# Backward pass of two attention and two gated feed-forward layers: the remaining turned gradient blocks come from transposing loads

## The chip, the cores and the metric

One program runs on one core of a Trainium2 chip. The core has TensorE (matmuls, PE in the profile, with its weight loads listed as PEld), VectorE (DVE), ScalarE (ACT), GpSimd (POOL) and SyncE (SP), which issues every transfer of this kernel from one queue (SPq); sixteen transfer engines carry the transfers out. The metric is the device time of one execution in microseconds, and lower is better. Matmul results land in PSUM, of which this kernel uses eight banks under the names t, g, u (two each), y and ln (one each).

## The reference

The reference runs a network of four layers forward and then returns the output and the gradients of the input and of all weights. It alternates a linear attention layer A and a gated feed-forward layer B, each behind a layer norm and with a residual. There are 2048 rows of 512 features, all in bf16.

```python
def _B_ref(x, w_gate, w_up, w_down):          # F = 1376
    g = jnp.einsum("bsd,df->bsf", x, w_gate)
    u = jnp.einsum("bsd,df->bsf", x, w_up)
    h = _sigmoid(g) * u
    return jnp.einsum("bsf,fd->bsd", h, w_down)
...
x = A_x
x = x + _A_ref(_layernorm(x, axis=-1), A_wqkv, A_wo)
x = x + _B_ref(_layernorm(x, axis=-1), B_w_gate, B_w_up, B_w_down)
x = x + _A_ref(_layernorm(x, axis=-1), A_wqkv, A_wo)
x = x + _B_ref(_layernorm(x, axis=-1), B_w_gate, B_w_up, B_w_down)
...
_out, _vjp = jax.vjp(_f, A_x, A_wqkv, A_wo, B_w_gate, B_w_up, B_w_down)
_grads = _vjp(grad_out)
```

The part that matters here is the gradient through `_B_ref`. With G the gradient of the layer's output, the gradient of h is G times w_down transposed. The matmul of TensorE contracts over the partitions, so G must be at hand turned, with its 512 features on partitions; this turned copy is the tile `gT`.

## The kernel before

The kernel runs the four layers forward and then backwards: the feed-forward gradient stage of layer 3 (the first such stage, 393 to about 500 us of the profile), the attention gradient of layer 2 with the weight gradients of layer 3 as filling, the feed-forward gradient stage of layer 1 (the second, from about 713 us), the attention gradient of layer 0, and the last weight gradients.

A feed-forward gradient stage is the class `BBwd`; its method `run` (L1507) goes through four blocks B of four row tiles each (512 rows), and in each block through eleven units u of 128 columns of F. Both stages together have eight blocks. For a unit, `D` (L1448) computes the gradient of h into a PSUM bank g (`dhh_ps`, four matmuls that stream all 512 rows of `gT`, L1461), ScalarE copies it to `dhb` (L1467), and VectorE and GpSimd multiply it with two factors `ssd` saved by the forward pass (L1468, L1469) into `dd`. `H` (L1485) then adds eight matmuls for that unit to four accumulators (`dh_ps`, L1493). `D` runs two units ahead of `H`. `R` turns `dd` on VectorE and stores it for the weight gradients (`tr_stg`, L1090, L1093). At a block's last unit `ln_begin` reads the four accumulators on ScalarE and VectorE (L1293, L1312), and the next block writes the same four banks. The loads of `ssd` come in groups of three units (two in the last) into two buffers (L1442), each load when the group two before it has been used; `h_ld` (L1446) is the saved row data for the layer norm's gradient, and `gstage` holds G in row layout.

There are two ways to fill `gT`, which has two buffers (and one more, `pre_gT`, for block 0 of the first stage). `turn_g` (L1407) issues two transposing loads of 256 rows each, from the input grad_out in the first stage (it is the gradient itself there) and from the stored rows `sv_gbf` in the second, which `cast_g` (L1415) has written. `make_gT` (L1423) turns 256 rows by eight TensorE transposes of `gstage` into a PSUM bank and one copy on ScalarE. Before the change the first stage uses loads for blocks 0 and 1 (`GTURN = 2`) and TensorE for blocks 2 and 3, in units 5 and 6 of block 1 and in units 7 and 8 of block 2; the second stage uses TensorE for block 0 and loads for blocks 1 to 3, each asked for at unit 0 of the block before.

The second stage begins while the weight gradients of layer 3 (`p2_gen`, L1722) still run. These are jobs of four units; a unit is sixteen matmuls into `p_ps` (L1778) and one copy out. A job reads a set `p_set` (L1655, L1662 or L1647) from two buffers; the next load of a set goes out when the job that used its buffer has ended. The last job is taken inside `run`: three units, then the transposes of block 0, then the fourth unit.

PE, ACT, DVE and POOL follow the order written in the program within these stages (`tc.manual_schedule(engines=EM)`). SP is not in that set: the framework places its transfers. `tc.issue_after` puts one transfer behind another by hand, as for the weights of the second stage (L247) and its first two `ssd` loads. The hook at block 1, unit 0 of the second stage (`open_w2`, L289) loads MT (L251) and the first sets of the next weight gradients.

Of the kernel before, what the change touches and what calls it, by code (L numbers as in the profile page):

```python
# [9 lines left out]
BF16 = mybir.dt.bfloat16  # L10
# [12 lines left out]
P = 128  # L23
NST = S // P
NDC = D // P
# [11 lines left out]
NBLK = NST // NB  # L37
BT = NB * P
# [22 lines left out]
def ps_tile(k, which, shape, dt, name):  # L61
    return k.ps[which].tile(shape, dt, name=name, tag="ln_tp" if which == "ln" else f"{which}_ps")
# [327 lines left out]
def dram_batch(ap2d, b, nb=NB):  # L390
    return ap2d[batch_rows(b, nb), :].rearrange("(n p) d -> p n d", p=P)
# [978 lines left out]
UNIT = [(g, u - c0, nch) for g, (c0, nch) in enumerate(CG) for u in range(c0, c0 + nch)]  # L1370


GTURN = 2


class BBwd:


# [18 lines left out]
    def load_g(self, B):  # L1397
        if B >= NBLK:
            return
        k, nc = self.k, self.k.nc  # L1400
        t = self.G[B] = self.G.get(B) or self.alloc(False, "stg", [P, NB, D], "gstage", 2)
        if self.first:
            if B < GTURN:
                self.turn_g(B)
            nc.sync.dma_start(out=t[:], in_=dram_batch(k.g_in, B))

# [8 lines left out]
    def cast_g(self, B, j):  # L1415
# [3 lines left out]
        nc.scalar.copy(self.G[B][:, j, :], k.xs[B * NB + j][:])  # L1419
        if j == NB - 1:  # L1420
            nc.sync.dma_start(out=dram_batch(self.sv["gbf"], B), in_=self.G[B][:])

    def make_gT(self, B, half, bank="ln"):  # L1423
        if B >= NBLK:
            return
        k, nc = self.k, self.k.nc
        if half == 0 and B not in self.gT:
            self.gT[B] = self.alloc(False, "work", [P, NDC, BT], "gT", 2)
        ps = ps_tile(k, bank, [P, NDC, 2, P], BF16, "gT_ps")
        for j in range(2):  # L1430
            for c in range(NDC):
                nc.tensor.transpose(ps[:, c, j, :], self.G[B][:, half * 2 + j, c * P:(c + 1) * P], k.ident[:])
        nc.scalar.copy(self.gT[B][:, :, half * 2 * P:(half + 1) * 2 * P], ps[:].rearrange("p c n t -> p c (n t)"))

    def load_ssd(self, n):
        B, g = divmod(n, len(CG))
# [70 lines left out]
    def run(self, nxt, hooks={}, rest=None, fill=None):  # L1507
        k, nc, tc, l = self.k, self.k.nc, self.k.tc, self.l
        if not self.first:
            k.load_b_weights([rest.R.dmas[i] for i in (-6, -5, -3, -3, -2, -1)])  # L1510
        with ExitStack() as ctx:
            for nm, bufs in (("ld", 2), ("stg", 2), ("work", 2), ("tr", 3)):
                self.p[nm] = ctx.enter_context(tc.tile_pool(name=f"bb_{nm}{l}", bufs=bufs, reuse_waits="tile"))
            self.small = ctx.enter_context(tc.tile_pool(name=f"bb_small{l}", bufs=4, reuse_waits="tile"))
            ctx.enter_context(tc.manual_schedule(engines=EM))
            if self.first:
                for n in (1, 2):
                    self.load_ssd(n)
            else:
                self.load_g(0)  # L1520
                with tc.issue_after(rest.R.dmas[-1]):
                    for n in range(2):
                        self.load_ssd(n)
                for j in range(NB):
                    self.cast_g(0, j)
                self.G[1] = self.alloc(False, "stg", [P, NB, D], "gstage", 2)
                for j in range(NB):
                    self.cast_g(1, j)
                if rest is not None:
                    rest.take(rest.left - 1)  # L1530
                self.make_gT(0, 0)
                self.make_gT(0, 1, "g")
                if rest is not None:
                    drain(rest)
            if self.first:
                self.load_g(1)
            for n in range(self.LOOK):
                self.D(n)
                self.R(n)
            self.D(self.LOOK)  # L1540
            self.R(self.LOOK)
            lns = None
            for B in range(NBLK):
                end = B == NBLK - 1
                for u in range(NFC):
                    n = B * NFC + u
                    close = u == NFC - 1
                    if close and end:
                        nxt.gT_make(0, "ln")
                    behind = self.first and B == 2 and u == 9  # L1550
                    if not close and not behind:
                        self.D(n + self.LOOK)
                    self.H(B, u)
                    if behind:
                        self.D(n + self.LOOK)
                    if close and not end:
                        done = self.ln_begin(B)
                        for i in range(2):
                            self.D(n + self.LOOK + i)
                    if u:  # L1560
                        self.R(n + self.LOOK)
                    if close and not end:
                        self.R(n + self.LOOK + 1)
                    if lns is not None:
                        for j, step in LNSTEPS[u]:
                            getattr(lns[j], step)()
                    if not end:
                        if not self.first and u == 0:
                            self.turn_g(B + 1)
                            if B + 2 < NBLK:  # L1570
                                self.load_g(B + 2)
                        if 1 <= u <= NB:
                            self.cast_g(B + 2, u - 1)
                        late = self.first and B == 2
                        if late and u == 3:
                            self.load_g(3)
                        if u in ((7, 8) if late else (5, 6)) and self.first and B + 1 >= GTURN:
                            self.make_gT(B + 1, 0 if u in (5, 7) else 1)
                    if u in (7, 8):
                        self.load_h(B, u - 7)  # L1580
                    if u == 8 and self.first and B != 1:
                        self.load_g(B + 2)
                    if (B, u) in hooks:
                        fill = hooks[B, u]() or fill
                    if end and u == 9:
                        nxt.begin()
                if not end:
                    lns = done
            lns = self.ln_begin(B, (0, 1))
            next(fill)  # L1590
            lns += self.ln_begin(B, (2, 3))
            nxt.gT_make(1, "ln")
            nxt.dp_make(0)
            next(fill)
            for x in lns:
                x.add()
            nxt.start()
# [14 lines left out]
def drain(gen):  # L1612
    for _ in gen:
        pass
# [575 lines left out]
```

## Time and profile before

| | us |
|---|---|
| median of 3 runs | 1104.92 (1104.79 to 1106.0) |
| the profiled execution | 1104.22 |
| its span, first to last instruction | 1102.5 |
| busy: TensorE, VectorE, ScalarE, GpSimd | 1076.6, 719.1, 484.9, 463.1 |
| transposes of `make_gT` (L1432) | 48 |
| its copies on ScalarE (L1433) | 6 |
| transposing loads of `turn_g` (L1412) | 10 |

In a timeline row the columns are the start in us from the span's start, the length in us, the engine, the line, the operation, the tiles written and read, the shape and the number of merged instructions; in square brackets stands the idle time of the engine before it and what ended it. SPq rows are issues: the length is the time that the queue was held by the issue, and the landing comes later. A row of a table by stretches has the stretch, the busy time of PE, PEld, DVE, ACT and POOL (with instructions), the granted clock of TensorE, the share of the sixteen transfer engines and GB/s.

### The profile page before, as it was taken

To read this page: it belongs to the slowest core of one execution; us is meant where nothing else is said; L and a number is where in the kernel's file an instruction comes from. 1 tells how busy PE (TensorE), PEld (TensorE's weight loads), DVE (VectorE), ACT (ScalarE), POOL (GpSimd) and SP (SyncE) were. 2 spreads that over 40 slices of the span, in tenths; PEclk is the share of its full clock that TensorE was granted. 3 is DMA by queue.
4 is the path that set the end of the run, shared out by engine and by line. 5 is a ranking of instruction groups with operands and counts; after the bars stand their busy time and mean duration, and the time that the engine had idled before them with its cause. 6 is when DMAs were issued, how large, how long until landed. Compare 5 with 4: busy or idle time off the path is not lost. (4 is left out here: it accounts for less than half of the span.)

```text
span 1102.5 us, 19826 instructions
## 1 busy us (share of the span) xinstructions
PE 1076.6 (98%) x7255; PEld 660.9 (60%) x7356; DVE 719.1 (65%) x1257; ACT 484.9 (44%) x907; POOL 463.1 (42%) x631
## 2 busy tenths in 40 slices
PE   8999999999999999999999999999999999999998
PEld 4477777447777744445756556544447755555587
DVE  7798997878888667777965620067778946632221
ACT  6676555547555524444633441234346513420001
POOL 5637776435765447773101420048881102420000
PEclk9999999999999999999999999999999999999999
DMA  8948997796797688976899968898869999958997
GB/s 260 318 150 216 249 251 231 208 251 155 219 290 230 188 273 287 300 237 209 244 269 258 273 212 283 253 334 250 233 189 247 272 256 264 263 184 285 266 253 168
DMA packets 365330, 269.55 MB, mean 244 GB/s; under 512 B 132464, under 2 KB 339760, under 8 KB 365232
## 3 DMA queue, kind: packets, MB, share of 16 engines
q1 hardware_dynamic: 365232, 268.28, 85.3%
q8 instruction: 57, 0.93, 0.3%
q14 instruction: 41, 0.34, 0.1%
HBM read 122.62 MB, written 119.47 MB: 220 GB/s over the span
## 5 line engine op out<-in xcount | busy, mean ns | idle before, releaser
L1778 PE MATMUL p_ps<-p_set,p_a 128*128 128x384 bf16 (+2 forms) x1792 | 264.4, 303 | 1.5 <-DMA p_set<-sv_hdd 0.8
L1778 PEld LDWEIGHTS <-p_a 128*128 128x128 bf16 x1792 | 168.8, 96 | 85.0 <-PE p_ps L1778 1.0
L1469 POOL TENSOR_TENSOR dd<-dhb,ssd 128x512 bf16<-128x512 bf16 x84 | 97.0, 1158 | 102.9 <-ACT dhb L1467 96.3
L1468 DVE TENSOR_TENSOR dd<-dhh_ps,ssd 128x512 bf16<-128x512 f32 x85 | 57.2, 679 | 119.9 <-ACT dhb L1467 117.1
L1493 PE MATMUL dh_ps<-wuT,dd 128*128 128x512 bf16 (+1 forms) x339 | 128.5, 379 | 0.5
L1493 PE MATMUL dh_ps<-wgT,dd 128*128 128x512 bf16 (+1 forms) x329 | 124.7, 379 | 0.1
L1493 PEld LDWEIGHTS <-dd 128*128 128x128 bf16 x680 | 66.4, 98 | 79.6
L1152 POOL TENSOR_TENSOR ssd_t<-hhT,oms 128x512 bf16<-128x512 bf16 (+2 forms) x76 | 82.8, 1098 | 49.1 <-DVE hhT L1151 22.4
L1793 DVE TENSOR_TENSOR dw_stg<-p_ps,dw_stg 128x384 bf16<-128x384 f32 (+2 forms) x76 | 32.2, 438 | 105.6 <-PE p_ps L1778 96.7
L1467 ACT CAST dhb<-dhh_ps 128x512 bf16<-128x512 f32 x84 | 48.7, 589 | 115.4 <-PE dhh_ps L1461 108.1
L1133 PE MATMUL u_ps<-hT,wu 128*128 128x256 bf16 (+1 forms) x792 | 92.7, 261 | 1.2 <-DVE hhT L1151 1.0
L1133 PE MATMUL g_ps<-hT,wg 128*128 128x256 bf16 (+1 forms) x792 | 92.8, 261 | 0.7 <-DVE den L972 0.4
L1090 DVE STREAM_TRANSPOSE tr_stg<-dd 128x768 f32<-128x768 f32 (+1 forms) x62 | 86.8, 1435 | 1.5 <-DMA sv_hdd<-tr_stg 0.4
L1133 PEld LDWEIGHTS <-wg 128*128 128x128 bf16 x792 | 70.1, 98 | 17.0 <-issue 0.5
L1461 PE MATMUL dhh_ps<-gT,wdT 128*128 128x512 bf16 x299 | 76.9, 379 | 2.2 <-DVE dd L1468 1.5
L1168 PE MATMUL y_ps<-wd,hhT 128*128 128x512 bf16 (+1 forms) x337 | 77.7, 379 | 0.8
L1133 PEld LDWEIGHTS <-wu 128*128 128x128 bf16 x792 | 70.6, 98 | 9.0 <-issue 2.1
L1149 ACT ACTIVATE ssd_t<-g_ps 128x512 bf16<-128x512 f32 (+2 forms) x76 | 42.5, 559 | 63.2 <-PE g_ps L1133 60.6
L1795 ACT CAST dw_stg<-p_ps 128x384 bf16<-128x384 f32 (+2 forms) x76 | 28.1, 386 | 84.1 <-PE p_ps L1778 80.9
L1461 PEld LDWEIGHTS <-wdT 128*128 128x128 bf16 x352 | 34.2, 98 | 43.3 <-issue 3.5
L1151 DVE TENSOR_TENSOR hhT<-u_ps,ssd_t 128x512 bf16<-128x512 f32 (+2 forms) x76 | 47.2, 629 | 17.8 <-PE u_ps L1133 11.0
L1150 ACT ACTIVATE oms<-g_ps 128x512 bf16<-128x512 f32 (+2 forms) x96 | 53.7, 559 | 10.0 <-POOL ssd_t L1152 9.3
(256 smaller groups left out, 1879.8 us busy)
## 6 DMA issues: line engine op xcount, KB each, us to landing
sv_hdd<-tr_stg SPq DMA_DIRECT2D x72, 384.0 KB, 4.8
p_set<-sv_hdd SPq DMA_DIRECT2D x18, 1536.0 KB, 7.3
ssd<-sv_ssd SPq DMA_DIRECT2D x23, 768.0 KB, 5.2
sv_ssd<-ssd_t SPq DMA_DIRECT2D x61, 256.0 KB, 3.4
h_ld<-sv_h SPq DMA_DIRECT2D x30, 256.0 KB, 4.0
sv_hdl<-tr_stg SPq DMA_DIRECT2D x24, 256.0 KB, 5.1
p_a<-sv_h SPq DMA_DIRECT2D x12, 512.0 KB, 6.7
p_set<-sv_hdl SPq DMA_DIRECT2D x24, 256.0 KB, 5.0
```

The costliest lines, as they stand in the source:

```text
L1090: nc.vector.transpose(t[:, :, 0:n * P].bitcast(F32).rearrange("p q (a j) -> p q a j", a=2 * n), src.rearrange("p c x -> p (c x)").bitcast( ...
L1133: nc.tensor.matmul(ps[:, ci * n:(ci + 1) * n], lhsT=w_sb[:, kc, (c0 + ci) * P:(c0 + ci + 1) * P], rhs=hT[:, kc, (st % 2) * P:(st % 2) * P ...
L1150: nc.scalar.activation(oms, gv, ACT.Sigmoid, scale=-1.0)
L1151: nc.vector.tensor_tensor(hh, uv, ssd[:, :, 0, :], ALU.mult)
L1152: nc.gpsimd.tensor_tensor(ssd[:, :, 1, :], hh, oms, ALU.mult)
L1168: nc.tensor.matmul(y_ps[:], lhsT=h[0:r, fc, off:off + P], rhs=k.wd[0:r, fc, :], start=(fc == 0), stop=(fc == NFC - 1))
L1461: nc.tensor.matmul(ps[:], lhsT=k.wdT[:, jc, u * P:(u + 1) * P], rhs=self.gT[B][:, jc, :], start=(jc == 0), stop=(jc == NDC - 1))
L1467: nc.scalar.copy(dhb[:], ps[:])
L1468: nc.vector.tensor_tensor(self.dd[ng][:, 0, c, :], ps[:], self.ssd[ng][:, c, 0, :], ALU.mult)
L1469: nc.gpsimd.tensor_tensor(self.dd[ng][:, 1, c, :], dhb[:], self.ssd[ng][:, c, 1, :], ALU.mult)
L1493: nc.tensor.matmul(self.acc[j][:], lhsT=dd[0:r, a, c, j * P:(j + 1) * P], rhs=w[0:r, u, :], start=(u == 0 and a == 0), stop=(u == NFC - 1 ...
L1778: nc.tensor.matmul(ps[:, 0:w], lhsT=lhs[:, s, ic * P:(ic + 1) * P], rhs=rhs, start=(s == 0), stop=(s == NST - 1))
```

## The change

`make_gT` and `GTURN` go. In the first stage blocks 0 and 1 are turned by loads as before; block 2's load is asked for in block 0 behind unit 3, and block 3's in block 2 behind unit 1. The special order of `D` and `H` at block 2, unit 9, goes too. In the second stage the four units of the last job are taken in a row, then block 0's turn is asked for by `turn_g`; blocks 1 to 3 stay as they were. The loads of G in row layout stay in both stages.

```diff
-GTURN = 2
...
-            if B < GTURN:
+            if B < 2:
                 self.turn_g(B)
...
-    def make_gT(self, B, half, bank="ln"):
-        if B >= NBLK:
-            return
-        k, nc = self.k, self.k.nc
-        if half == 0 and B not in self.gT:
-            self.gT[B] = self.alloc(False, "work", [P, NDC, BT], "gT", 2)
-        ps = ps_tile(k, bank, [P, NDC, 2, P], BF16, "gT_ps")
-        for j in range(2):
-            for c in range(NDC):
-                nc.tensor.transpose(ps[:, c, j, :], self.G[B][:, half * 2 + j, c * P:(c + 1) * P], k.ident[:])
-        nc.scalar.copy(self.gT[B][:, :, half * 2 * P:(half + 1) * 2 * P], ps[:].rearrange("p c n t -> p c (n t)"))
...
-                if rest is not None:
-                    rest.take(rest.left - 1)
-                self.make_gT(0, 0)
-                self.make_gT(0, 1, "g")
-                if rest is not None:
-                    drain(rest)
+                rest.take(NDC)
+                self.turn_g(0)
+                drain(rest)
...
-                    behind = self.first and B == 2 and u == 9
-                    if not close and not behind:
+                    if not close:
                         self.D(n + self.LOOK)
                     self.H(B, u)
-                    if behind:
-                        self.D(n + self.LOOK)
...
-                        late = self.first and B == 2
-                        if late and u == 3:
+                        if self.first and (B, u) in ((0, 3), (2, 1)):
+                            self.turn_g(2 + B // 2)
+                        if self.first and B == 2 and u == 3:
                             self.load_g(3)
-                        if u in ((7, 8) if late else (5, 6)) and self.first and B + 1 >= GTURN:
-                            self.make_gT(B + 1, 0 if u in (5, 7) else 1)
```

## The prediction

> **What bounds the kernel now.** I read the page first, for the engine that sets the time.
>
> ```profile
> span 1102.5 us, 19826 instructions
> ...
> PE 1076.6 (98%) x7255; PEld 660.9 (60%) x7356; DVE 719.1 (65%) x1257; ACT 484.9 (44%) x907; POOL 463.1 (42%) x631
> ```
>
> TensorE is busy 98% of the span at a granted clock of 1.00 in all stretches read, so an instruction taken from it is worth its place in its row of work, and a wait put into that row costs its length. The other lists matter where they make TensorE wait. Next, TensorE's timeline around the transposes that go (first stage, then start of the second):
>
> ```profile
> 435.44 0.61 PE L1432 MATMUL gT_ps<-ident,gstage 128*128 128x128 bf16 x8
> 435.89 1.03 PE L1461 MATMUL dhh_ps<-gT,wdT 128*128 128x512 bf16 x4
> ```
> ```profile
> 709.30 1.05 PE L1432 MATMUL gT_ps<-ident,gstage 128*128 128x128 bf16 x16
> 710.20 2.80 PE L1778 MATMUL p_ps<-p_set,p_a 128*128 128x384 bf16 x16
> 712.83 1.89 PE L1461 MATMUL dhh_ps<-gT,wdT 128*128 128x512 bf16 x7
> ```
>
> The second number is pipelined length; what counts is the distance of starts: 0.45 us for eight transposes (435.44 to 435.89), 0.90 us for sixteen (709.30 to 710.20). No idle time stands before any of them.
>
> Third, the transfer queue, SP's timeline, in the stretch before the second stage, and one row far ahead of it:
>
> ```profile
> 649.47 2.83 SPq L1421 DMA_DIRECT2D sv_gbf<-gstage  x2
> ...
> 655.81 0.51 SPq L247 DMA_DIRECT2D wdT<-wdT_d  x1
> 662.66 0.36 SPq L1655 DMA_DIRECT2D p_set<-sv_hdd  x1
> ...
> 702.68 0.84 SPq L1647 DMA_DIRECT2D p_set<-sv_dq  x1
> 703.62 5.74 SPq L1412 DMA_TRANSPOSE gT<-sv_gbf  x2
> ```
> ```profile
> 565.03 0.44 SPq L251 DMA_DIRECT2D MT<-sv_MT  x1
> ```
> ```profile
> 669.71 10.55 PE L1778 MATMUL p_ps<-p_set,p_a 128*128 128x384 bf16 x63 [0.79 <-DMA p_set<-sv_hdd]
> ```
>
> Two things are to be seen. The queue does not keep the written order: the load of MT at 565.03 is written in the hook of block 1, unit 0 of the second stage, which TensorE reaches near 743, and it went out as soon as its buffer was free. And the p_set load of 662.66 is already late: it lands 6.9 us after issue, at 669.6, and TensorE stood 0.79 us for it. Whatever delays it further is paid in full.
>
> Fourth, the queue at the start of the first stage, and the one VectorE row that its last load releases:
>
> ```profile
> 398.98 2.60 SPq L1412 DMA_TRANSPOSE gT<-in_grad_out_dram  x2
> 401.67 0.54 SPq L1405 DMA_DIRECT2D gstage<-in_grad_out_dram  x1
> ...
> 406.74 2.67 SPq L1446 DMA_DIRECT2D h_ld<-sv_h  x2
> 409.46 0.56 SPq L1405 DMA_DIRECT2D gstage<-in_grad_out_dram  x1
> 410.13 0.56 SPq L1442 DMA_DIRECT2D ssd<-sv_ssd  x1
> ```
> ```profile
> 417.44 0.69 DVE L1468 TENSOR_TENSOR dd<-dhh_ps,ssd 128x512 bf16<-128x512 f32 x1 [1.03 <-DMA ssd<-sv_ssd]
> ```
>
> From 398.98 to 410.69 the queue has no pause over 0.1 us, and each transfer lands 5 to 7 us after its issue. The ssd load of 410.13 lands 7.2 later, at 417.3, and VectorE waits for it. Last, what a turn costs the transfer engines:
>
> ```profile
> 401.40:406.60 5.20, 5.20 (x25) 2.34 (x24) 4.21 (x4) 1.17 (x2) 2.29 (x3) 1.00 1.04 261
> 709.50:712.60 3.10, 3.10 (x31) 2.13 (x29) 0.00 (x0) 2.37 (x3) 0.00 (x0) 1.00 1.13 119
> 662.40:664.60 2.20, 2.20 (x24) 2.07 (x22) 0.00 (x0) 0.80 (x3) 0.00 (x0) 1.00 0.35 63
> ```
>
> The last two columns are the transfer engines' share and GB/s. In 709.5:712.6, after the p_set load of 702.68 has landed (6.9 later) and until the second half-turn of 707.5 has (5.1 later), they are full with one block's turn (512 KB): 3.1 us. In 401.4:406.6 a turn and a plain 512 KB load of gstage share 5.2 us; a plain gstage load takes about 1.45 (the h_ld of 408.17 lands at 413.8, the gstage load behind it at 415.2), which leaves 3.7. So a turn holds the full transfer engines for 3.1 to 3.7 us, over twice its plain load.
>
> **The change part by part.**
>
> TensorE, removed. Two blocks of the first stage and one of the second, two halves each: 6 × 0.45 = 2.7 us, all on the path. ScalarE loses six copies of 1.01 us; it is 44% busy, and in these rows TensorE waits for none of them, so nothing. D and H at block 2, unit 9 go back to the common order; no idle stands there on TensorE (470 to 475): nothing.
>
> [...] This trace has 56 ns of TensorE (0.90 / 16) and 194 ns of the transfer engines (3.1 / 16). [...]
>
> Second stage, block 0's turn (two transposes, L1412) added. Where does it go out? Block 1's turn shows it: its rows landed by 655.3 (second store 651.92, 3.4 later), yet it went out at 703.62. What it lacked was, I infer, its turn for a gT buffer: block 0 takes the first, and block 0's is written by ScalarE's copy near 710 in the written order. Now block 0's own turn is a transfer with its rows landed at 652.4 (649.47 + 2.9), and both turns are free to go like MT did: when the queue is next idle, at 656.4, behind the wdT load and ahead of the p_set load that waits for TensorE until 662.66. Two turns are 6.2 us of transfer. The loads before them land until 662.4 (wdT, 655.81 + 6.6); then the turns until 668.6. The p_set's data flowed from 664.6 to 669.6 (share 0.35 before that); now they start at 668.6: 4.0 us late, and so is TensorE. Ends: the four transposes may take the queue 1.25 each (first stage), which leaves the issue at 662.66 alone, and at 1.45 us a turn the data would be 0.7 late; or 3.87 and 1.82 twice (703.62's rows), issue at 667.8, data 1.9 later (as 662.66 to 664.6), 5.1 late; with the slowest row, 4.27 four times, 10.7. I take 4.0, nearest to the rows with a full queue. TensorE meets the first D with gT long landed: nothing there. Behind the p_set in the queue stand a store and the next p_set, due 11 us later: nothing.
>
> First stage, block 2's turn at block 0, unit 3. Its buffer is the second one, free like the first. Written after unit 3's stores and ahead of the h loads (units 7 and 8), it comes at the latest where these went out, 406.74. Behind it wait two h loads, gstage and the ssd load of 410.13, all in a full queue, so ssd lands 3.1 to 3.7 later. Unit 11's product on VectorE waits with it, and behind that in VectorE's order the four sums of the block's end, which free the accumulators; the last sum ends at 421.84 and TensorE uses its accumulator at 421.8. VectorE's slack before the sums is 0.36 (418.13 to 418.50). So 2.7 to 3.3 on the path; 1.3 to 1.9 if the queue's order puts ssd ahead of gstage (1.45 less); nothing, if the turn stands behind ssd. I take 2.7, by the purer of the two turn rows.
>
> First stage, block 3's turn: its buffer is free after block 1's last D, near 445, so it goes out after the p_a loads, about 448.7, in a pause of the queue until 454.0. It may make that ssd load (454.01, landing 5.1 later) 1.5 us later, due at 462.5: nothing, and at most 1.5 if that cover were gone.
>
> Sum: -2.7 + 4.0 + 2.7 = +4.0 us. The profiled execution took 1104.22 us (1102.5 and 1.7 around it), so 1108.2; the median of three, 1104.92, lies 0.7 above it, so 1108.9 there.
>
> **Rivals.**
>
> All hidden (the other side): the turns go out in pauses, in the second stage between 673 and 680 or 683 and 691, in the first behind ssd. For it: the queue has these pauses. Against: a free transfer goes out at the first pause. It decides from 0.5 us of new waits downwards: -2.7, 1102.2.
>
> One stall alone: the second stage's (-2.7 + 4.0, 1106.2) or the first's (-2.7 + 2.7, 1104.9). For it: the two are 250 us apart and rest on different orders.
>
> Late turn: block 0's turn of the second stage keeps its written place. At 703.62's place it lands at 712.6, wanted at 711.9: 0.7, with the first stage's 2.7 1105.6. Behind the last store (713.98) it would land near 723 by the same rows: 11 us, 1115.9. Against: MT.
>
> A turn is no dearer than a plain load: 1.45 us of transfer. Then 0.7 in the second stage, 1.1 in the first (1.45 - 0.36): -0.9, 1104.0. The rows' 3.1 and 3.7 speak against it. [...]
>
> **How the numbers follow.** Both stalls 0.42; one alone 0.22; all hidden 0.22; late 0.09; as cheap as plain 0.05. 0.2% (2.2 us) is about what a measurement here can tell from no change. Slower by more: 0.40 of the first, 0.02 of one alone, 0.04 of late, 0.46. Faster: all hidden and a little of the cheap turn, 0.24. Within: 0.30. The range must hold both signs: from all hidden, 1101.9, to 1111.5, which covers the first stage's 3.3 and 5.9 of the second's stall. The likeliest's own range is 1106.5 to 1111.5.
>
> **What would show it.** No L1432; L1412's first rows of the second stage near 656; the p_set issue of 662.66 later, and the 0.79 wait near 4.8; four transposes of L1412 before 411 where there are two, and VectorE's 1.03 wait on ssd near 4, with TensorE idle after it near 420. Wrong: if these waits stay as they were and TensorE's count falls by 48, all is hidden; if dhh_ps waits for gT, the turn was late.

## The result, and the profile after

The changed kernel takes 1118.28 us (median of four, 1117.25 to 1121.12); the kernel before, run beside it, 1104.86. The ratio is 1.0125, 95% interval 1.0113 to 1.0137: 13.4 us slower, where 4.0 slower were forecast, and 6.8 us above the top of the range. The profiled execution took 1118.08 us. Its page, the lines that answer to the first two shown of before:

```profile
span 1116.4 us, 19734 instructions
...
PE 1079.4 (97%) x7208; PEld 660.2 (59%) x7308; DVE 718.5 (64%) x1257; ACT 479.1 (43%) x901; POOL 462.5 (41%) x631
```

The 48 transposes and the six copies are gone, yet TensorE is busy 2.8 us longer than before (1079.4 against 1076.6) and the span is 13.9 us longer. Less work with more busy time is the first sign that something made the work itself slower; more on that below. The waits of TensorE, the four that concern the change (total, times, longest):

```profile
PE p_ps L1756 <- DMA p_set<-sv_hdd: 5.7, 1, 5.7
PE dh_ps L1478 <- DVE junk L1312: 4.5, 2, 3.1
...
PE dhh_ps L1446 <- DVE dd L1453: 2.2, 5, 0.5
PE p_ps L1756 <- DVE dw_stg L1771: 1.7, 3, 0.6
```

The first was 0.79 before. The second did not exist: TensorE now waits twice for the sums at a block's end. In the list of after, line numbers are up to 22 lower than before: `turn_g` is L1409, `D` L1446, `H` L1478, `ssd` L1427, `h_ld` L1431, `p_ps` L1756.

**End of block 0 of the first stage.** The transfer queue, then the VectorE rows that wait for it:

```profile
407.91 5.00 SPq L1409 DMA_TRANSPOSE gT<-in_grad_out_dram  x2
412.96 0.59 SPq L1431 DMA_DIRECT2D h_ld<-sv_h  x1
413.66 0.39 SPq L1427 DMA_DIRECT2D ssd<-sv_ssd  x1
...
415.42 1.10 SPq L1431 DMA_DIRECT2D h_ld<-sv_h  x1
```
```profile
419.10 0.69 DVE L1453 TENSOR_TENSOR dd<-dhh_ps,ssd 128x512 bf16<-128x512 f32 x1 [1.91 <-DMA ssd<-sv_ssd]
...
422.97 0.75 DVE L1312 SCALAR_TENSOR_TENSOR junk<-dh_ps,rstd_all,h_ld 128x512 bf16<-128x512 f32 x1 [1.65 <-DMA h_ld<-sv_h]
```

Block 2's turn holds the queue from 407.91 to 412.91, ahead of the h loads, and the ssd load that went out at 410.13 before goes out at 413.66. VectorE waits 1.91 us for it (1.03 before) and then another 1.65 for the second h load.

**End of block 1.** The queue (first fence), VectorE (second) and TensorE (third):

```profile
446.34 0.34 SPq L1427 DMA_DIRECT2D ssd<-sv_ssd  x1
446.97 1.50 SPq L1093 DMA_DIRECT2D sv_hdl<-tr_stg  x2
448.56 0.63 SPq L1431 DMA_DIRECT2D h_ld<-sv_h  x1
```
```profile
455.28 0.75 DVE L1312 SCALAR_TENSOR_TENSOR junk<-dh_ps,rstd_all,h_ld 128x512 bf16<-128x512 f32 x1 [3.66 <-DMA h_ld<-sv_h]
```
```profile
456.09 0.38 PE L1478 MATMUL dh_ps<-wuT,dd 128*128 128x512 bf16 x1 [3.05 <-DVE junk L1312]
456.31 0.38 PE L1478 MATMUL dh_ps<-wgT,dd 128*128 128x512 bf16 x1
...
457.56 1.44 PE L1446 MATMUL dhh_ps<-gT,wdT 128*128 128x512 bf16 x3 [0.44 <-DVE dd L1453]
459.22 0.63 PE L1478 MATMUL dh_ps<-wuT,dd 128*128 128x512 bf16 x1 [0.22 <-issue]
459.64 0.63 PE L1478 MATMUL dh_ps<-wgT,dd 128*128 128x512 bf16 x1
```

The same two loads in the queue of before:

```profile
442.02 0.74 SPq L1446 DMA_DIRECT2D h_ld<-sv_h  x1
444.48 0.34 SPq L1442 DMA_DIRECT2D ssd<-sv_ssd  x1
```

Before, block 1's second h load went out 2.5 us ahead of the ssd load. Now it goes out at 448.56, 2.2 us behind ssd and behind two stores, and lands at 455.16. The sums of the block's end wait 3.66 us for it, and TensorE 3.05. The rows of `H` show the second sign: 0.22 us from start to start at 456.09, 0.42 at 459.22.

**Second stage.** The queue, and TensorE:

```profile
662.57 0.68 SPq L247 DMA_DIRECT2D wdT<-wdT_d  x1
663.29 9.10 SPq L1409 DMA_TRANSPOSE gT<-sv_gbf  x4
672.50 0.52 SPq L1633 DMA_DIRECT2D p_set<-sv_hdd  x1
```
```profile
680.82 24.36 PE L1756 MATMUL p_ps<-p_set,p_a 128*128 128x384 bf16 x132 [5.70 <-DMA p_set<-sv_hdd]
```

Everything is some 6 us later than before because of the first stage. The order is the one forecast: both turns directly behind the wdT load, ahead of the p_set load, which lands 8.2 us after its issue, at 680.7.

**The clock.** A table by stretches (stretch, length, busy time of PE, PEld, DVE, ACT, POOL, granted clock, share of the transfer engines, GB/s):

```profile
453.74:457.15 3.41, 1.02 (x4) 0.38 (x4) 1.77 (x5) 0.00 (x0) 0.36 (x3) 1.00 1.43 279
457.16:460.57 3.41, 2.79 (x7) 1.06 (x8) 3.38 (x4) 0.58 (x1) 3.41 (x5) 0.50 0.60 128
675.61:679.02 3.41, 0.00 (x0) 0.00 (x0) 0.00 (x0) 0.00 (x0) 0.00 (x0) 1.00 0.98 316
679.02:685.85 6.83, 5.03 (x16) 2.30 (x17) 0.00 (x0) 0.00 (x0) 0.00 (x0) 0.50 1.06 380
```

TensorE is granted half its clock for 3.41 us after the stall at block 1's end and for 6.83 us after the stall on the p_set. The profiled execution of before has no such stretch inside the run.

**Where the time went.** I matched each instruction of VectorE, ScalarE and GpSimd with the same one of the other profile and took the median shift of the starts over every 10 us of before. The shift moves in steps:

| us of before | step | what lies there |
|---|---|---|
| 10, 240, 630 | +0.4, +0.5, +0.4 | no wait of the change; the first two lie ahead of it |
| 420 | +2.0 | end of block 0: ssd, then h |
| 440, 470, 710 | -0.9, -1.0, -0.9 | the transposes that are gone |
| 450 | +3.6 | end of block 1: h |
| 460 | +1.5 | half clock for 3.41 us |
| 670 | +7.3 | p_set 4.9 later (5.70 - 0.79), half clock 2.4 |
| 1050, 1090 | +0.8, +0.8 | `p_ps` waits for `dw_stg` in the last weight gradients |

### The profile page after: what moved, and what is told of

Read it like the earlier page. It is cut to its first block, busy times and chain, and to the rows that moved or that the text cites. A ratio compares the mean times of both kernels' runs of the same rounds, so it can differ in the third digit from the quotient of the medians.

```text
span 1116.4 us, 19734 instructions
## 1 busy us (share of the span) xinstructions
PE 1079.4 (97%) x7208; PEld 660.2 (59%) x7308; DVE 718.5 (64%) x1257; ACT 479.1 (43%) x901; POOL 462.5 (41%) x631
## 5 line engine op out<-in xcount | busy, mean ns | idle before, releaser
L1756 PE MATMUL p_ps<-p_set,p_a 128*128 128x384 bf16 (+2 forms) x1792 | 266.7, 305 | 7.0 <-DMA p_set<-sv_hdd 5.7
L1756 PEld LDWEIGHTS <-p_a 128*128 128x128 bf16 x1792 | 169.5, 96 | 92.5 <-issue 9.2
L1478 PE MATMUL dh_ps<-wuT,dd 128*128 128x512 bf16 (+1 forms) x339 | 129.0, 380 | 5.2 <-DVE junk L1312 4.5
L1478 PE MATMUL dh_ps<-wgT,dd 128*128 128x512 bf16 (+1 forms) x329 | 125.0, 380 | 0.1
L1478 PEld LDWEIGHTS <-dd 128*128 128x128 bf16 x680 | 66.7, 98 | 85.4 <-issue 6.5
L1446 PE MATMUL dhh_ps<-gT,wdT 128*128 128x512 bf16 x300 | 77.6, 381 | 2.8 <-DVE dd L1453 2.2
L1446 PEld LDWEIGHTS <-wdT 128*128 128x128 bf16 x352 | 34.5, 98 | 44.9 <-issue 4.7
```

Of the source, the lines that this page charges most:

```text
L1446: nc.tensor.matmul(ps[:], lhsT=k.wdT[:, jc, u * P:(u + 1) * P], rhs=self.gT[B][:, jc, :], start=(jc == 0), stop=(jc == NDC - 1))
L1478: nc.tensor.matmul(self.acc[j][:], lhsT=dd[0:r, a, c, j * P:(j + 1) * P], rhs=w[0:r, u, :], start=(u == 0 and a == 0), stop=(u == NFC - 1 ...
L1756: nc.tensor.matmul(ps[:, 0:w], lhsT=lhs[:, s, ic * P:(ic + 1) * P], rhs=rhs, start=(s == 0), stop=(s == NST - 1))
```

## The experiments

Theory after the result: the two queue mechanisms of the prediction hold, and three terms are missing from the sum: a second stall at block 1's end, caused by block 2's turn; the half clock that follows a stall; and something at the end of the run. Ten kernels were run; the medians of before beside them were 1104.5 to 1104.6.

### One stage at a time

The kernel before with only the second stage changed:

```diff
-                if rest is not None:
-                    rest.take(rest.left - 1)
-                self.make_gT(0, 0)
-                self.make_gT(0, 1, "g")
-                if rest is not None:
-                    drain(rest)
+                rest.take(NDC)
+                self.turn_g(0)
+                drain(rest)
```

> The kernel before with the change's second stage alone (the last job's four units in a row, block 0 turned by loads). Theory: the p_set load behind the two turns makes TensorE wait 5.7 us where it waited 0.8, and the granted clock is then half for some 6.8 us, which costs 2.4 more: 4.9 + 2.4 - 0.9 for the transposes = +6.4, 1111.3 us, clock below 1.00. Rival (the forecast's own sum, a wait costs its length alone): +4.0 - 0.9 or with the measured wait 4.9 - 0.9, so 1108.0 to 1108.9 with the clock at 1.00.

Measured: 1111.09 us (1109.53 to 1116.69), ratio 1.0068 (1.0041 to 1.0095). Queue, TensorE and the stretch ahead of the half clock:

```profile
656.09 8.31 SPq L1412 DMA_TRANSPOSE gT<-sv_gbf  x4
664.51 0.51 SPq L1652 DMA_DIRECT2D p_set<-sv_hdd  x1
```
```profile
673.14 32.17 PE L1775 MATMUL p_ps<-p_set,p_a 128*128 128x384 bf16 x184 [4.50 <-DMA p_set<-sv_hdd]
```
```profile
670.56:673.97 3.41, 0.83 (x6) 0.51 (x7) 0.00 (x0) 0.00 (x0) 0.00 (x0) 1.00 1.05 392
```

Half clock follows from 673.97 to 677.39 (mean granted clock of this execution 0.998). The step of the shift at 670 is 5.4 us: 3.7 of added wait (4.50 - 0.79) and 1.7 for 3.41 us at half rate. This is the forecast's stall, 3.7 for 4.0, with a second price behind it. The wait and the half clock are smaller than expected here (4.9 and 2.4), and with the transposes gone they leave 4.5 us; the profiled execution loses 2.3 us more, at 800 (0.5) and in small steps behind 1040 (1.8), which no term stands for. So the median's agreement with 1111.3 is in part luck.

The whole change without its second stage, which keeps the transposes of before (`make_gT` comes back for it):

```diff
-                rest.take(NDC)
-                self.turn_g(0)
-                drain(rest)
+                if rest is not None:
+                    rest.take(rest.left - 1)
+                self.make_gT(0, 0)
+                self.make_gT(0, 1, "g")
+                if rest is not None:
+                    drain(rest)
```

> The kernel before with the change's first stage alone (blocks 2 and 3 turned by loads, TensorE still turns block 0 of the second stage). Theory: waits of 1.9 us at the end of block 0 and 3.5 us at the end of block 1, half clock for some 3.4 us behind the second (1.5 more), 1.8 us of transposes saved: +5.2, 1110.1 us. Rival (the forecast: the end of block 1 costs nothing): +2.0 - 1.8, 1105.1 us.

Measured: 1111.66 us (1108.86 to 1115.02), ratio 1.0065 (1.004 to 1.0091). Both ends of blocks stall TensorE (2.09 and 3.02 us, and each time 0.44 more), and here both are followed by 3.41 us of half clock, from 425.1 and from 459.2. The stretches ahead of these:

```profile
421.70:425.11 3.41, 1.30 (x6) 0.54 (x6) 2.45 (x6) 0.00 (x0) 1.04 (x3) 1.00 1.08 363
455.84:459.24 3.40, 1.47 (x7) 0.59 (x7) 2.62 (x6) 0.00 (x0) 1.21 (x3) 1.00 1.23 228
```

The profiled execution took 1115.02, the longest of the four; two others took 1108.86 and 1109.58 at a higher mean granted clock (0.998 and 0.999 against 0.997), so two half-clock stretches are not this kernel's rule. Each stage alone costs some 7 us, and the two medians together lie 13.6 us above before, which is the whole change's 13.4. Within these intervals nothing suggests that the stages interact.

### Which turn stalls block 1's end

Block 2's turn alone, block 3's left to TensorE:

```diff
+                        if self.first and (B, u) == (0, 3):
+                            self.turn_g(2)
...
-                        if u in ((7, 8) if late else (5, 6)) and self.first and B + 1 >= GTURN:
+                        if u in ((7, 8) if late else (5, 6)) and self.first and B + 1 > GTURN:
```

> The kernel before with block 2's turn alone moved to a load behind unit 3 of block 0; block 3 and the second stage keep TensorE. Theory (the turn, and the units 5 and 6 that lose their transposes, change the order in which the framework places the h loads, so each block's second h load goes out behind ssd and the stores): both waits stay, 1.9 at the end of block 0 and 3.5 at the end of block 1, and half clock behind at least one of them, 1.5; with 0.9 saved +6.0, 1110.6 us. Rival (the wait at the end of block 1 comes from block 3's turn, which is not in this kernel): +1.9 - 0.9, 1105.6 us and no wait near 456.

Measured: 1111.72 us (1110.57 to 1115.14), ratio 1.0066 (1.0048 to 1.0084). Queue, VectorE and TensorE at block 1's end:

```profile
446.13 0.34 SPq L1442 DMA_DIRECT2D ssd<-sv_ssd  x1
448.34 1.42 SPq L1446 DMA_DIRECT2D h_ld<-sv_h  x1
```
```profile
454.42 0.75 DVE L1312 SCALAR_TENSOR_TENSOR junk<-dh_ps,rstd_all,h_ld 128x512 bf16<-128x512 f32 x1 [3.01 <-DMA h_ld<-sv_h]
```
```profile
455.23 0.38 PE L1493 MATMUL dh_ps<-wuT,dd 128*128 128x512 bf16 x1 [2.40 <-DVE junk L1312]
```

The stall is there without block 3's turn. The rival that block 3's turn makes it falls: block 2's turn, 40 us earlier, is enough, and the h load again stands behind ssd. The half clock that was expected did not follow in the profiled execution (1110.57 us), where the clock is 1.00; the other three had mean clocks of 0.998, 0.997 and 0.996 and took 1110.73, 1112.70 and 1115.14 us. Is that order the cause, or merely a companion? The same kernel with the h loads written one unit earlier:

```diff
-                    if u in (7, 8):
-                        self.load_h(B, u - 7)
+                    if u in (6, 7):
+                        self.load_h(B, u - 6)
```

> The same as block 2's turn alone, but the h loads are written one unit earlier (units 6 and 7), which puts block 1's second h load ahead of ssd again and leaves block 0's order as it was with the turn. Theory: the wait at the end of block 1 goes, the one at the end of block 0 stays: +1.9 - 0.9, and 1.7 more where the clock falls: 1105.6 to 1107.3 us. Rival (the waits come from the transfer time of the turn, not from the order of the h loads): no better than block 2's turn alone, 1110.6 us.

Measured: 1107.90 us (1105.93 to 1111.77), ratio 1.0032 (1.002 to 1.0044), 3.8 us under the kernel without that edit.

```profile
444.74 0.76 SPq L1446 DMA_DIRECT2D h_ld<-sv_h  x1
446.74 0.34 SPq L1442 DMA_DIRECT2D ssd<-sv_ssd  x1
```
```profile
452.28 0.75 DVE L1312 SCALAR_TENSOR_TENSOR junk<-dh_ps,rstd_all,h_ld 128x512 bf16<-128x512 f32 x1 [0.25 <-DMA h_ld<-sv_h]
```

With the h load ahead of ssd again, VectorE waits 0.25 us and TensorE not at all, though the turn is the same. So the late place of the h load is the cause of the stall at block 1's end. In the profiled executions the step there falls from 2.9 to 0.2 us, the one at block 0's end grows from 2.2 to 3.1, and the rest of the gain lies later, without a cause that a run shows. The stall at block 0's end stays (TensorE 2.17 us): there the turn itself stands ahead of the loads. Why the framework turned the two loads round in block 1 is not shown by any run, and the turn was not separated there from the transposes that left units 5 and 6 of that block.

### Are the bytes dear, or the turning?

The kernel before, with four plain loads of the same 1 MB into the two gT buffers where the turns would stand:

```diff
+                for i in range(2):
+                    self.gT[i] = self.alloc(False, "work", [P, NDC, BT], "gT", 2)
+                    v = self.gT[i][:].rearrange("p c t -> p (c t)").rearrange("p (n d) -> p n d", n=NB)
+                    for half in range(2):
+                        nc.sync.dma_start(out=v[:, 2 * half:2 * half + 2, :],
+                                          in_=dram_batch(self.sv["gbf"], 2 * i + half, 2))
...
-                            self.turn_g(B + 1)
+                            if B == 0:
+                                with tc.issue_after(rest.R.dmas[-1]):
+                                    self.turn_g(1)
+                            else:
+                                self.turn_g(B + 1)
```

> The kernel before, with plain loads of the same 1 MB of gradient rows (blocks 0 and 1 of the second stage) added where the change sends its turns; they fill the gT buffers and are overwritten by the transposes as before, block 1's turn is held behind the last set. Theory (a turned load is what costs: 3.1 to 3.7 us a block against 1.45): the p_set load is 0.7 us later, TensorE waits about 1.5 us, the clock stays at 1.00: 1105.6 us. Rival (any 1 MB at this place delays the set as much): the wait is 5 us or more as in the changed kernel and the time 1110 to 1112 us.

Measured: 1104.49 us (1103.11 to 1105.75), ratio 0.9999 (0.9990 to 1.0008).

```profile
656.27 2.92 SPq L1535 DMA_DIRECT2D gT<-sv_gbf  x4
662.54 0.37 SPq L1665 DMA_DIRECT2D p_set<-sv_hdd  x1
```
```profile
670.10 35.14 PE L1788 MATMUL p_ps<-p_set,p_a 128*128 128x384 bf16 x212 [1.29 <-DMA p_set<-sv_hdd]
```

The same bytes in the same place hold the queue for 2.92 us instead of 8.31, the p_set load keeps its place at 662.5, and TensorE's wait grows by 0.5 us instead of 3.7. It is the turning that costs.

### Does the half clock follow from TensorE's idle time?

The kernel with the second stage alone, and twenty matmuls on TensorE ahead of the job that comes late:

```diff
+        if (nm, final, c0) == ("wd", False, CG[1][0] * P):
+            junk = ps_tile(k, "y", [P, 512], F32, "warm_p2")
+            for _ in range(20):
+                nc.tensor.matmul(junk[:], lhsT=lhs[:, 0, 0:P], rhs=lhs[:, 0, :], start=True, stop=True)
```

> The same as the second stage alone, with 20 matmuls of 512 columns whose results nobody reads (20 x 0.216 = 4.3 us) put on TensorE just ahead of the job whose set is late. Theory (the half clock follows from TensorE's idle time): the idle time left is about 1.4 us, the clock stays at 1.00 and the job runs at full speed: 2.4 us less than the second stage alone, 1108.9 us, though TensorE does more. Rival (the half clock comes from something else, such as the full transfer engines): the clock falls as before and the time is that of the second stage alone, 1111.3 us, or more.

Measured: 1107.72 us (1106.76 to 1111.31), ratio 1.0035 (1.0022 to 1.0047).

```profile
668.97 4.48 PE L1774 MATMUL warm_p<-p_a 128*128 128x512 bf16 x20
674.28 31.01 PE L1779 MATMUL p_ps<-p_set,p_a 128*128 128x384 bf16 x187 [0.83 <-DMA p_set<-sv_hdd]
```

The p_set comes as late as without them, TensorE does 4.5 us more of work whose result nobody reads, and the median is 3.4 us lower (the two intervals still touch: 1.0041 and up against 1.0047 and down). In the profiled execution the clock stays at 1.00 until the work is done. By their mean clocks, six of the eight executions had 0.999 or 1.000, and the two with 0.998 were the longest (1111.08 and 1111.31); the four without the twenty matmuls had 0.998 or less. The transfers beside it are the same (the four half-turns hold the queue 8.40 us against 8.31, the p_set load goes out at 665.07 against 664.51), so the drop follows from TensorE's idle time.

### Every turn out of the way of what is urgent

If it is only the place in the queue that costs, a turn held behind what is urgent should leave the gain. First the second stage alone, with block 0's turn behind the last set load (block 1's followed it):

```diff
+                rest.take(NDC)
+                with tc.issue_after(rest.R.dmas[-1]):
+                    self.turn_g(0)
+                drain(rest)
```

> The kernel before with the change's second stage, but with both of its turns held behind the load of the last set (about 691). Theory: the set that was late is not touched, the turns land near 708 to 711, before TensorE wants them at 711.9: 0.9 saved, 1103.7 us, clock at 1.00. Rival (the turns are late for the first unit behind two ssd loads in a full queue): TensorE waits 1 to 4 us ahead of the first dhh_ps, 1105 to 1108 us.

Measured: 1106.15 us (1103.36 to 1107.86), ratio 1.0006 (0.9997 to 1.0016). The p_set wait is 0.86 and the 0.89 of the transposes is won at 710, as expected, but 1.3 is lost again near 743, at the end of block 0, where TensorE now stands three times, 0.15, 0.27 and 0.66 us. VectorE waited there 2.79 us for an earlier store of `tr_stg` to land. Another 2.1 us are lost from 800 on, which no run here explains. The waits of the rival did not come either, only its time.

Then all eight turned by loads, the added ones held (block 2's behind block 1's third ssd load, at 426.73 us, block 3's behind block 2's third, at 455.76), and the h loads one unit earlier. Against the changed kernel:

```diff
...
-                self.turn_g(0)
+                with tc.issue_after(rest.R.dmas[-1]):
+                    self.turn_g(0)
...
-                        if self.first and (B, u) in ((0, 3), (2, 1)):
-                            self.turn_g(2 + B // 2)
+                        if self.first and (B, u) in ((0, 10), (2, 1)):
+                            with tc.issue_after(self.last_ssd):
+                                self.turn_g(2 + B // 2)
...
-                    if u in (7, 8):
-                        self.load_h(B, u - 7)
+                    if u in (6, 7):
+                        self.load_h(B, u - 6)
```

> All eight blocks turned by loads as in the change, with every added turn held out of the way: block 2's behind block 1's second ssd load (about 426), block 3's behind block 2's third (about 456), the second stage's behind the last set (about 691); h loads written one unit earlier. Theory (the change lost by place and order alone): no new wait, 2.7 us of transposes saved, 1101.9 us, faster than before by 0.24%. Rival (the transfer engines are full anyway, so a turn of 3 us delays something wherever it goes): waits on ssd or h loads remain and the time is 1104 us or more.

Measured: 1104.37 us (1103.06 to 1107.18), ratio 0.9998 (0.9989 to 1.0007). No stall over 0.5 us is left in the first stage, and the shift against before falls to -1.6 us by 470 and -1.9 from 710 to 1040. The three steps of the transposes (0.9, 1.0 and 0.9) are what the sum said; 0.7 of them is lost near 570, where the same code lost nothing in the execution profiled in the next section. The theory's 1101.9 did not come: the time is the rival's, though not by its waits on ssd and h loads. Behind 1040 the lead goes:

```profile
1055.80 6.46 PE L1758 MATMUL p_ps<-p_set,p_a 128*128 128x224 bf16 x64 [1.25 <-DVE dw_stg L1773]
1062.64 3.31 PE L1758 MATMUL p_ps<-p_set,p_a 128*128 128x224 bf16 x32 [0.37 <-DVE dw_stg L1773]
...
1094.96 3.65 PE L1758 MATMUL p_ps<-p_set,t_a 128*128 128x256 bf16 x32 [1.23 <-DVE dw_stg L1773]
```

### The end of the run

`dw_stg` is filled by VectorE, which adds a partial sum that comes by a load. That load of wu landed at 1052.8 before and at 1053.2 here, though TensorE was 1.9 us ahead; ahead of it and behind it in the queue stand four turned loads of X. To see whether the queue holds the end, those four became plain loads of the same bytes (X is then not turned, and the last weight gradient is not the right one), with the held turns and, as a control, in the kernel before:

```diff
-                    yield k.nc.sync.dma_start_transpose(out=T[nm, l][:, :, r], in_=src[r, :])
+                    if nm == "XT":
+                        yield k.nc.sync.dma_start(out=T[nm, l][:, 2 * i:2 * i + 2, :],
+                                                  in_=src[r, :].rearrange("(c p) d -> p c d", p=P))
+                        continue
+                    yield k.nc.sync.dma_start_transpose(out=T[nm, l][:, :, r], in_=src[r, :])
```

> All eight blocks turned by loads, the added turns held, the h loads one unit earlier, as in the kernel that came out level with before; and the four turned loads of X near the end replaced by plain loads of the same 1 MB, so that the last weight gradient is computed from X unturned. Theory: TensorE reaches 1040 us 1.9 us ahead of before and loses it because the loads of partial sums and of the last p_set land no earlier than before, behind the turned loads of X on a queue that has no room there. With plain loads those land some 3 to 4 us earlier, so the waits of p_ps for dw_stg near 1056 and 1063 (1.25 and 0.37 us) go, and the time is 1.0 to 1.9 us under before: 1102.6 to 1103.5. Rival, the gain is lost between 1040 and the end for a reason that has nothing to do with the queue (VectorE's adds, or chance of the single execution): the waits stay and the time is 1104.0 to 1104.8, level with before and with the companion run.

> The kernel before with only the four turned loads of X near the end replaced by plain loads of the same bytes (the last weight gradient is then computed from X unturned). Theory: before, TensorE waited only 0.27 and 0.40 us between 1040 us and the end, so there is at most 0.7 us to win: 1103.8 to 1104.5, and the other kernel's lead over this one is 1 us or more. Rival, relief of the queue is worth the same to both kernels: both come out the same amount under before.

Measured: with the held turns 1103.56 us (median of eleven), but from 1100.38 to 1108.31, ratio 0.9999 (0.9987 to 1.0011); the control 1104.69 (1103.61 to 1106.22), ratio 1.0000 (0.9991 to 1.0009). The profiled execution of the first is its fastest, 1100.38. There the lead of 2.8 us at 1040 is kept and ends at 3.4, and after 1035 TensorE's only listed wait is

```profile
PE p_ps L1758 <- DMA p_set<-sv_dq: 0.3, 1, 0.3
```

The load of wu's partial sum went out at 1043.52 instead of 1046.62 and landed at 1050.6:

```profile
1043.52 1.11 SPq L1714 DMA_DIRECT2D dw_stg<-dwp_wu  x1
```
```profile
1046.62 0.45 SPq L1714 DMA_DIRECT2D dw_stg<-dwp_wu  x1
```

(the second row is of the held turns without the edit). In that one execution the theory's steps are all to be seen; the eleven times do not bear it out as a rule, since executions up to 1108 are among them that no profile shows. That the queue takes back the lead at the end stays a reading of single traces. The control shows that relief there is worth nothing to the kernel before. No version was faster than before by its interval.

## Why the prediction was wrong

**The direction was right, and so were the first steps of both mechanisms.** The framework took the second stage's turns as soon as their rows and buffers allowed, behind wdT and ahead of the urgent p_set load; block 2's turn went ahead of the h loads; VectorE waited for ssd and TensorE behind it. `dhh_ps` never waited for `gT`, so no turn was late. The likeliest case came, and its sum was wrong. Term by term, from the profiled execution:

| term | forecast | measured |
|---|---|---|
| transposes gone | -2.7 | -2.8 |
| second stage, p_set later | +4.0 | +4.9 (+3.7 with that stage alone) |
| end of block 0 | +2.7 | +2.0 |
| end of block 1 | nothing | +3.6 |
| half clock after the stalls | not in the sum | +1.5 and +2.4 |
| steps ahead of the change, at 630 and at the end | not in the sum | +2.9 |

The steps add up to 14.5 us, against 13.9 of span and 13.4 of medians.

**The step that failed in the first stage** is "Behind it wait two h loads, gstage and the ssd load of 410.13". It was followed to the end of block 0 and no further. The prediction had itself shown that the queue does not keep the written order, and used that for where the turns go; it did not ask what the new transfer does to the order of others. With block 2 alone turned by a load, block 1's second h load changes places with ssd, and that costs more than the stall that was priced. Block 3's turn, forecast at nothing, adds at most the 0.6 us by which the step at 450 is smaller without it (2.9 against 3.5 with the first stage alone). At block 0's end the forecast had VectorE's wait for ssd near 4 us, and it was 1.91, 0.9 more than before, because ssd went out ahead of the second h load and gstage. The other part was a wait of 1.65 for that h load, displaced by the same turn. So +2.0 for +2.7 is near by luck: the load that cost most there is not the one that was priced.

In the second stage the size was right, but not by full transfer engines alone: with that stage alone the four turned loads held the queue itself until 664.40, so the p_set load went out at 664.51 instead of 662.66 and landed 8.5 us after its issue instead of 6.9.

**The missing term** is the clock. The prediction read 1.00 in all stretches and concluded that a wait "costs its length". In this kernel it costs more: the p_set stall cost 4.9 of waiting and 2.4 of half rate. The run with the twenty matmuls bears it out: both kernels get the p_set late, and the one whose profile shows no half clock has a median 3.4 us lower, with intervals that touch. The trace of the other puts 1.7 us on one stretch. The range missed for this reason as much as for block 1: its ends held every stall at its length.

**The cheap-turn rival falls.** A turned 1 MB held the queue 8.31 us, a plain one 2.92. The sum's 3.1 to 3.7 us of transfer for a turn came nearer, but the issues were priced too loosely: the four transposes took 9.10 us here where the rows of before gave 5.0 (four of 1.25) to 11.4 (3.87 and 1.82, twice).

**All hidden falls as it was put**, since the free transfers went out at the first pause (the second stage's at 663.29 us). Put there by hand, the turns were hidden almost wholly, and 1.9 us of the sum's 2.7 were left at 1040. The lead then did not reach the end of the run, which the prediction took for granted with "all on the path". By the reading of single traces above, a gain in the middle is worth its length only as far as the next place where transfers set the time.

Three figures of the working do not hold, and none of them moves the outcome. The loads from 398.98 on landed 3.5 to 7.2 us after their issue, not 5 to 7. The stretch 709.50:712.60 moved 0.37 MB by its 119 GB/s, not the whole 512 KB of a turn; the price of about 3 us a turn was right all the same, since with the second stage alone the four half-turns landed 1.3 to 1.7 us apart. And all hidden is 1102.2 as a rival but 1101.9 as the end of the range.

## What to carry to other kernels

A transfer that is added to a full queue must be priced twice: by what stands behind it, and by which other loads change their order because of it; compare the whole queue of the two kernels up to the end of the stage, not only the neighbours. When a change makes TensorE wait for two microseconds or more, add the half clock that may follow (in the profiled executions it followed waits of 2.09, 3.02, 3.05, 4.50 and 5.70 us, and did not follow waits of 2.17 and 2.40), and look at whether a few matmuls in the gap whose result nobody reads pay (with 4.48 us of them the median was 1107.72 us, without 1111.09). Turned loads cost about three times the queue time of plain ones here (8.31 us against 2.92 for 1 MB), so hold them behind what is urgent.

## What the runs showed of the hardware

The half-clock stretches inside the run are whole multiples of one length. In the clock record of the trace of after they are 3.413 and 6.827 us, and the full-clock stretches behind them 218.453 and 430.079, which are 64.0 and 126.0 times 3.413; with the first stage alone the two begin at 425.11 and 459.24, 34.13 apart, 10.0 times 3.413. These lengths fit a clock that changes on a fixed grid of 3.413 us and not from the start of a wait; that is a reading of these traces, which no run tested by itself. In them the half clock goes with what TensorE did in the grid's stretch ahead: 0.00, 0.83, 1.02, 1.30 and 1.47 us of busy time in it (up to 43%) were followed by half clock, the last four with single waits of 4.50, 3.05, 2.09 and 3.02 us. With block 2's turn alone, two waits of 1.67 and 2.40 us fell so that the grid's stretches kept more, and the clock stayed full:

```profile
420.06:423.47 3.41, 1.84 (x9) 0.74 (x8) 1.67 (x6) 1.74 (x6) 0.45 (x3) 1.00 1.06 395
...
450.78:454.19 3.41, 2.05 (x10) 0.83 (x9) 0.63 (x2) 1.95 (x6) 0.24 (x2) 1.00 1.09 345
454.19:457.61 3.42, 1.88 (x8) 0.82 (x9) 3.05 (x7) 0.00 (x0) 1.68 (x4) 1.00 0.46 175
```

In these eight stretches the boundary lies between 1.47 and 1.84 us of 3.41. Other stretches of the grid narrow it: 1.73 us (the h loads early, from 420.20) and 1.49 were followed by full clock. The last is the stretch ahead of the one of 0.83 us, with the second stage alone:

```profile
667.15:670.56 3.41, 1.49 (x16) 1.20 (x13) 0.00 (x0) 0.77 (x4) 0.00 (x0) 1.00 0.98 311
```

So the boundary lay near 1.5 us here at full clock; in the profile after, 1.61 us of busy time at half clock (from 679.02) were followed by half clock again. A wait of 2.40 us with a grid line in its midst cost nothing extra. One of 2.09 cost 1.7 us (half of the 3.41 behind it): 1.67 of it fell in one stretch, and the wait of 0.44 behind it too. The grid's place differs from run to run (the clock record's first full-clock stretch begins at 4.24 us in the profile before and at 6.60 in the one after, 2.36 apart), so the same kernel can pay in one execution and not in another: the four executions with block 2's turn alone have mean clocks from 1.000 to 0.996, and the lower the clock, the longer the time. That may be why the stalled kernels' times spread over 4 to 7 us and those of before over 3.4 at most, but it is not all: the held turns with plain loads of X spread over 7.9 us, and their longest execution, 1108.31, has a mean clock of 1.000.
